# Scores ahead of the transposes in each step: one block moved in a fused attention and mixture-of-experts kernel

## The chip, the cores and the metric

The kernel runs on one core of one Trainium2 chip. Its time is the device time of one execution in microseconds (us). Several executions are run, and their median is quoted. A separate execution was taken by the hardware profiler; every duration of a single instruction below comes from that one. The engines are named as in the profile: PE is the matrix engine (TensorE), PEld its weight loads, DVE is VectorE, ACT is ScalarE, POOL is GpSimd and SP is SyncE, which here only issues DMA transfers.

## The reference

Two layers are computed, one after the other. The first is attention over 8 batches, 8 heads, 576 positions and 64 dimensions, in a causal window of 128 positions with a distance penalty. The second is a mixture of 8 experts over all 4608 tokens of 512 values, with a dense branch added.

```python
scores = scale * np.matmul(q, k.transpose(0, 1, 3, 2))
mask = (rel >= 0) & (rel < window)                       # window = 128
scores = np.where(mask, scores + bias[None], -1000000000.0)
attn = np.exp(scores - np.max(scores, axis=-1, keepdims=True))
attn = attn / (np.sum(attn, axis=-1, keepdims=True) + 1e-09)
x = np.matmul(attn, v)                                   # then to (4608, 512)

y_dense = np.maximum(x @ w1_dense, 0.0) @ w2_dense
logits = x @ w_gate
expert_idx = np.argmax(logits, axis=1)
gate_w = softmax(logits)[np.arange(N), expert_idx]
for e in range(8):                                       # each token by its one expert
    y_moe[mask] = gate_w[mask, None] * (np.maximum(x[mask] @ w1[e], 0.0) @ w2[e])
return y_dense + y_moe
```

## The kernel before

**Two stages.** In the first stage (to about 286 us) attention, the dense branch and the routing run together. In the second, 43 blocks of 128 rows go through the experts: `block` gathers the rows by DMA, does two layers and scatters the sum to the output. The dense pieces of the last batch run between the first blocks.

**Steps.** The first stage is a loop over 48 steps, `steps = [(u, pr) ...]`. A unit `u` is half the heads of one batch, so a batch is two units and six steps. A unit has three steps: `pr` 0 and 1 handle two blocks of 128 keys each (tiles of 128x1024 for two pairs of heads), `pr` 2 the last, short block (tiles of 128x128). The work on one pair `(u, pr)` is spread over several passes of the loop:

- In pass n, `scores` (L384) puts the mask and the key-query products of step n into two PSUM tiles `sq` (16 matmuls at L405, then 16 or 8 at L417), and ACT turns each into `p32` by one `Exp` (L428). The function `lo` that it returns subtracts the upper half of the bits on DVE (`plo`, L447). It is called at the end of the pass.
- In pass n+1, `attend` (L458) multiplies these by V into the one PSUM tile `ax` (L481: 48, 36 or 24 matmuls).
- In pass n+2, `norm` (L490) divides by the sums on DVE (L496, L497). This frees `ax`.
- In pass n+3, `flip` (L511) transposes the result on PE into a PSUM tile `tp` (L524) and ACT copies `tp` twice: to `xT` in fp32 for the routing and to `xTb` in bf16 for the dense branch (L531).

**Work between.** `items` and `gates` hold the routing and the dense branch of the batch that was last finished, cut into pieces. In pass n the first item runs between `norm` and `attend`, the others behind `attend`. Over the six passes of a batch they are: the gate product `gate_a` (`lp`, L546) and its reader on DVE `gate_av` one pass later; `gate_b` (`lg`, L571); `gate_c` (`pc`, L605, L613), read by `gate_d` one pass later; eight `dense1` (`hp`, L691, four matmuls each, read by ACT's `Relu` at L698); five `dense2` (`yp`, L706, read by ACT's copy at L714 and then scattered by POOL, L715).

**PSUM.** `sq` has one buffer for each of its two tiles and `ax` has one. All of `tp`, `lp`, `lg`, `pc`, `hp` and `yp` come from one pool, `psum_m`, with the tag `misc` and two buffers. A buffer is handed on when the last reader of its tile has been written down in the program; the instruction that fills it next waits for that reader. So while `lp` or `pc` waits for its reader in the next pass, one buffer alone goes round.

**Order.** The queues of PE, ACT and DVE stand exactly in the order in which the Python code emits them (`manual_schedule`, L1010), as does SP's queue up to pass 48 (L1027). POOL's order is chosen by the framework's scheduler. At the end of a pass stand the loads and turns of the next units: `turn` on DVE (L162), and on ACT `round_qk`, which makes `kT` (L172, in `pr` 1) and `qT` (L169, in `pr` 2). `qT` has a single buffer, and the scores of the next unit's `pr` 0 read it.

Of the kernel before, what the change touches and what calls it, by code (L numbers as in the profile page):

```python
# [23 lines left out]
def kernel(  # L24
# [100 lines left out]
    def load_k(u):  # L125
        b, hq = divmod(u, HQ)
        t = ld.tile([P, R, 2, 32], F32, name="kraw", tag="kraw")
        nc.sync.dma_start(
            out=t.rearrange("p r c d -> p (r c d)"),
            in_=k[b, 4 * hq : 4 * hq + 4].rearrange("h (p r) d -> (h p) (r d)", r=R),  # L130
        )
        raw[("k", u)] = t
# [26 lines left out]
    def turn(u, nm):  # L159
        t = raw.pop((nm, u))  # L160
        s = stg.tile([P, 2, S], F32, name=f"{nm}s", tag=f"{nm}s")
        nc.vector.transpose(out=s.rearrange("p c (r x) -> p r c x", r=R), in_=t)  # L162
        tmp[(nm, u)] = s

    def round_qk(u, nm):
        s = tmp.pop((nm, u))
        if nm == "q":
            d = qtp.tile([P, 2, S], F32R, name="qT", tag="qT", bufs=1)
            nc.scalar.copy(out=d, in_=s)  # L169
        else:  # L170
            d = kTs[u % 2]
            nc.scalar.copy(  # L172
                out=d[:, :, 0:S].rearrange("p c (x r) -> p c x r", r=R),
                in_=s.rearrange("p c (r x) -> p c x r", r=R),
            )
        qkT[(nm, u)] = d
# [69 lines left out]
    def mask_consts():  # L246

        nc.vector.tensor_single_scalar(
            out=far_i, in_=d_i, scalar=7, op=ALU.logical_shift_right
        )  # L250
        nc.vector.scalar_tensor_tensor(
            out=dist, in0=far_i, scalar=FAR, in1=d_i, op0=ALU.mult, op1=ALU.max
        )

        ax = psum_ax.tile([P, 2, 512], F32, name="ax", tag="ax")
        hp = psum_m.tile([P, 512], F32, name="hp", tag="misc")
        turned.extend((dist, ax[:, 0, :], ax[:, 1, :], hp))
        for g in range(1, 4):
            nc.tensor.matmul(
                out=turned[g],  # L260
                lhsT=ident2[:, P - 32 * g : 2 * P - 32 * g],
                rhs=dist,
                start=True,
                stop=True,
            )
# [3 lines left out]
    def mask_head(h):  # L269
        slope = 2.0 ** (-8.0 * (h + 1) / H)  # L270
        nc.scalar.activation(
            out=mask[:, h, :], in_=turned[h % 4], func=ACT.Copy, scale=-slope / SCALE
        )

    def mask_rest():
        for h in range(4, H):
            mask_head(h)
# [447 lines left out]
    def dense_items(b):  # L725
        one = [lambda c=c, h=h: dense1(b, c, h) for h in range(2) for c in range(4)]
        two = [lambda t=t: dense2(b, t) for t in range(NT)]
        return [one[0:2], one[2:4], two[0:2], one[4:6], one[6:8], two[2:5]]
# [10 lines left out]
    steps = [(u, pr) for u in range(NU) for pr in range(3)]  # L739
    NS = len(steps)  # L740
# [269 lines left out]
    with tc.manual_schedule(engines={ENG.PE, ENG.Activation, ENG.DVE}):  # L1010
        mask_consts()
        turn(0, "k")
        for h in range(4):
            mask_head(h)
        round_qk(0, "k")
        more_constants()
        mask_rest()
        turn(0, "q")
        round_qk(0, "q")
        load_k(1)  # L1020
        load_q(1, nc.sync)
        norms, gates, items = {}, {}, {}
        wnext = 0
        jm = 0
        n = 0
        loads = ExitStack()
        loads.enter_context(tc.manual_schedule(engines={ENG.SP}))  # L1027
        while jm < NB:
            if n == NS:
                loads.close()  # L1030
            if n > NS + 1:
                def middle():
                    if n - 2 in norms:
                        norms.pop(n - 2)()
                    for f in gates.pop(n, []):
                        f()
                    if n - 3 < NS:
                        flip(*steps[n - 3])

                block(jm, [middle] + items.pop(n, []))  # L1040
                jm += 1
            if 0 <= n - 3 < NS:
                if n <= NS + 1:
                    flip(*steps[n - 3])
                u2, pr2 = steps[n - 3]
                b2 = u2 // HQ
                if pr2 == 2:
                    items.setdefault(n, []).append(lambda u=u2: gate_a(u))
                    gates.setdefault(n + 1, []).append(lambda u=u2: gate_av(u))
                if u2 % HQ == HQ - 1 and pr2 == 2:  # L1050
                    for i, f in ((1, gate_b), (2, gate_c)):
                        items.setdefault(n + i, []).append(lambda f=f, b=b2: f(b))
                    for i, f in ((2, gate_bv), (3, gate_d)):
                        gates.setdefault(n + i, []).append(lambda f=f, b=b2: f(b))
                    for i, fs in enumerate(dense_items(b2)):
                        items.setdefault(n + 2 + i, []).extend(fs)
                    if b2 == NQ - 1:
                        gen = route_early()
                        for i in range(5):
                            gates.setdefault(n + 4 + i, []).append(  # L1060
                                lambda g=gen: next(g, None)
                            )
                        gates.setdefault(n + 9, []).append(early_used)
                    if b2 == B - 1:
                        gen = late_table()
                        part = lambda: next(gen, None)
                        for i, f in enumerate(
                            (late_counts, part, late_fill, part, part, part)
                        ):
                            gates.setdefault(n + 4 + i // 2, []).append(f)  # L1070
            lo = None
            if n < NS:
                u, pr = steps[n]
                lo = scores(u, pr)
            if n - 2 in norms:
                norms.pop(n - 2)()
            for f in gates.pop(n, []):
                f()
            if n == 0:
                prep_v(0)  # L1080
            todo = items.pop(n, [])
            for f in todo[:1]:
                f()
            if 0 <= n - 1 < NS:
                norms[n - 1] = attend(*steps[n - 1])
            for f in todo[1:]:
                f()
            if n < NS:
                if pr == 0:
                    if u + 1 < NU:  # L1090
                        turn(u + 1, "k")
                        if u + 2 < NU:
                            load_k(u + 2)
                elif pr == 1:
                    if u + 1 < NU:
                        round_qk(u + 1, "k")
                        turn(u + 1, "q")
                        if u + 1 + 1 < NU:
                            load_q(u + 1 + 1, nc.sync)
                else:  # L1100
                    if u + 2 < NU:
                        load_v(u + 2)
                    if u + 1 < NU:
                        round_qk(u + 1, "q")
                        prep_v(u + 1)
            if lo:
                lo()
            if n == 0:
                load_v(1)
            while wnext < 2 * (E + 1) and n < NS and wnext <= 18 * (n - 4) / 42:  # L1110
                pace(wnext)
                load_weights(wnext)
                wnext += 1
            if n == NS + 1:
                ph1.close()
                mpool = ctx.enter_context(
                    tc.tile_pool(name="mpool", bufs=3, reuse_waits="tile")
                )
                psum_t, psum_h, psum_y = [
                    ctx.enter_context(  # L1120
                        tc.tile_pool(
                            name=nm,
                            bufs=2,
                            space=bass.MemoryType.PSUM,
                            reuse_waits="tile",
                        )
                    )
                    for nm in ("psum_t", "psum_h", "psum_y")
                ]
                for j in range(AHEAD + 1):  # L1130
                    fetch(j)
            n += 1
        assert wnext == 2 * (E + 1)
# [30 lines left out]
```

## Time and profile before

| What | Value |
|---|---|
| Median of 3 executions | 434.8 us (432.84 to 435.57) |
| The profiled execution: its time | 435.34 us |
| Its span, first to last instruction | 433.6 us |
| Busy share of the span: PE, PEld, DVE, ACT, POOL | 81%, 51%, 65%, 60%, 46% |
| Mean granted PE clock | 0.93 of full speed |
| `Exp` of a 128x1024 tile (L428) | 1025 ns, 64 of them |
| Copy of a 128x512 `tp` to `xT`, to `xTb` (L531) | 588 ns, 596 ns, 32 of each |
| `plo` of a 128x1024 tile (L447) | 1236 ns, 64 of them |
| First `xr` load of the second stage issued by SP | 288.54 us |

In the lines shown further on, a timeline row has the start in us, the duration of the merged run in us, engine, source line, operation and tiles, the count, and in brackets the idle time of the engine before the row with what ended it. A waits row reads "engine, tile, line <- what it waited for: us in total, times, longest". A windows row has a stretch of the span, its length, and for each engine the busy us with the count of instructions, then the granted clock, the DMA share and GB/s. Matmuls are pipelined and their ends are modelled, so the runs of neighbouring matmuls overlap a little.

### The profile page before, as it was taken

What the parts mean: (1) busy time and instruction counts of PE and PEld (TensorE: products, weight loads), DVE (VectorE), ACT (ScalarE), POOL (GpSimd) and SP (SyncE); (2) the same over time, 40 slices, a digit from 0 to 9 for tenths busy, and PEclk for the clock granted to TensorE, in tenths of its full rate; (3) what the DMA queues carried; (4) which work ended last, traced back from release to release, by engine and by line L of the source; (5) the groups of instructions that cost most, each with busy time, mean ns of one, the idle gap of its engine ahead of it and who ended that gap; (6) DMA issues with size and microseconds to landing.
All of it is one profiled execution on the core that took longest, in us unless ns stands there. A gap on an engine that the chain in (4) does not pass through costs nothing.

```text
span 433.6 us, 12269 instructions
## 1 busy us (share of the span) xinstructions
PE 350.9 (81%) x4659; PEld 220.0 (51%) x4659; DVE 279.7 (65%) x541; ACT 261.1 (60%) x431; POOL 197.6 (46%) x245
## 2 busy tenths in 40 slices
PE   3547689898897898879879878758949899999990
PEld 0435466556566456466556545533525455555550
DVE  5579987788787788577887969711425244454440
ACT  6538854787786787467687677533424555555550
POOL 4023134445764665644567554360453534444341
PEclk9969985999899998889999899996988999999997
DMA  4657687878777969669669573138768789889820
GB/s 143 178 129 156 165 166 159 226 162 207 212 176 218 224 162 234 169 193 216 130 190 217 200 178 50 63 126 286 241 218 295 251 245 290 242 245 249 281 98 13
DMA packets 84986, 82.40 MB, mean 190 GB/s; under 512 B 43583, under 2 KB 71615, under 8 KB 84928
## 3 DMA queue, kind: packets, MB, share of 16 engines
q1 hardware_dynamic: 66852, 48.17, 39.9%
q0 software_dynamic: 17680, 33.12, 30.0%
q8 instruction: 38, 0.62, 0.6%
q10 hardware_dynamic: 396, 0.33, 0.2%
q14 instruction: 20, 0.16, 0.1%
HBM read 64.20 MB, written 28.66 MB: 214 GB/s over the span
## 4 chain that ended last, share of the span: by engine, by line
PE 35%; DVE 14%; issue 13%; DMA 12%; POOL 9%; ACT 6%; another core or an unknown queue 5%; SPq 2%; POOLq 1%; ACTq 0%; DVEq 0%
PE ax L481 8%; POOL out_dram L975 8%; DVE plo L447 8%; PE yp L706 6%; DMA qraw<-in_q_dram 6%; PE hp L691 5%; PE tp L524 3%; DMA vf<-in_v_dram 3%; ACT p L428 3%; PE sq L417 3%; DVE qs L162 2%; DVE xf L497 2%; PE lp L546 2%; PE lg L571 2%
## 5 line engine op out<-in xcount | busy, mean ns | idle before, releaser
L447 DVE TENSOR_TENSOR plo<-p 128x1024 bf16<-128x1024 f32 (+1 forms) x96 | 86.5, 941 | 26.5 <-ACT p L428 22.1
L428 ACT ACTIVATE p<-sq 128x1024 f32<-128x1024 f32 (+1 forms) x96 | 69.7, 783 | 22.8 <-remote 6.2
L481 PE MATMUL ax<-vf,p 128*128 128x65 bf16 (+1 forms) x576 | 69.6, 206 | 16.8 <-DVE xf L497 13.4
L481 PEld LDWEIGHTS <-p 128*128 128x128 bf16 (+1 forms) x1152 | 65.7, 108 | 29.9 <-DVE xf L497 17.4
L975 POOL DMA_INDIRECT out_dram<-yo,xr x43 | 42.4, 986 | 75.8 <-DVE yo L974 66.8
L503 POOL CAST xrow<-xf 128x512 bf16<-128x512 f32 (+1 forms) x48 | 34.9, 732 | 81.5 <-DVE xf L497 75.1
L481 PE MATMUL ax<-vl,p 128*128 128x64 bf16 (+1 forms) x576 | 68.9, 203 | 1.9 <-issue 1.8
L481 PE MATMUL ax<-vf,plo 128*128 128x65 bf16 (+1 forms) x576 | 69.0, 204 | 0.9 <-issue 0.6
L715 POOL DMA_INDIRECT ys_dram<-yt,slot x40 | 48.0, 1200 | 27.3 <-ACT yt L714 17.7
L481 PEld LDWEIGHTS <-plo 128*128 128x128 bf16 (+1 forms) x576 | 59.3, 107 | 1.6 <-issue 1.0
L691 PE MATMUL hp<-xTb,w_all 128*128 128x256 bf16 (+1 forms) x256 | 45.8, 308 | 14.3 <-ACT hTd L698 6.8
L966 PE MATMUL y<-w_all,hTm 128*128 x172 | 45.3, 386 | 8.1 <-ACT hTm L958 7.3
L924 DVE COPY xTm<-xps 128x512 bf16<-128x512 bf16 x43 | 18.2, 424 | 51.7 <-PE xps L918 29.6
L645 POOL DMA_INDIRECT xs_dram<-xrow,slot x40 | 43.1, 1077 | 17.0 <-issue 11.1
L698 ACT ACTIVATE hTd<-hp 128x256 bf16<-128x256 f32 (+1 forms) x64 | 26.6, 418 | 39.8 <-PE hp L691 31.7
L939 PE MATMUL hpm<-w_all,xTm 128*128 x172 | 45.7, 389 | 2.7 <-DVE xTm L924 1.2
L974 DVE TENSOR_TENSOR yo<-y,yr 128x512 f32<-128x512 f32 x43 | 29.7, 691 | 23.8 <-PE y L966 21.4
L706 PE MATMUL yp<-w_all,hTd 128*128 128x512 bf16 (+1 forms) x160 | 42.4, 393 | 1.9 <-DVE ltsb L560 1.0
L947 ACT ACTIVATE hr<-hpm,xr 128x512 bf16<-128x512 f32 x43 | 29.6, 687 | 21.9 <-PE hpm L939 10.5
L958 ACT COPY hTm<-hps 128x512 bf16<-128x512 bf16 x43 | 25.1, 585 | 28.4 <-PE hps L954 23.6
L531 ACT COPY xT<-tp 128x512 f32<-128x512 f32 (+1 forms) x48 | 23.1, 482 | 23.1 <-PE tp L524 19.7
L524 PE MATMUL tp<-ident_f,xf 128*128 128x128 f32 (+1 forms) x160 | 27.6, 289 | 11.3 <-ACT yt L714 6.6
(146 smaller groups left out, 573.3 us busy)
## 6 DMA issues: line engine op xcount, KB each, us to landing
yr<-ys_dram SPq DMA_DIRECT2D x43, 256.0 KB
kraw<-in_k_dram SPq DMA_DIRECT2D x16, 576.0 KB
vf<-in_v_dram SPq DMA_DIRECT2D x64, 128.0 KB
w_all<-in_moe_w_dram POOLq DMA_DIRECT2D x16, 512.0 KB
qraw<-in_q_dram SPq DMA_DIRECT2D x62, 128.0 KB
xr<-xs_dram SPq DMA_DIRECT2D x43, 130.0 KB
ys_dram<-fill_x SPq DMA_DIRECT2D x8, 256.0 KB
xs_dram<-fill_x SPq DMA_DIRECT2D x8, 130.0 KB
```

Of the source, the lines that this page charges most:

```text
L428: nc.scalar.activation(out=p32[:, :, 0:tot], in_=sq[i][:, :, 0:tot], func=ACT.Exp, scale=SCALE,)
L447: nc.vector.tensor_tensor(out=plo[:, :, 0:tot], in0=p32[:, :, 0:tot], in1=phi[:, :, 0:tot], op=ALU.subtract,)
L481: nc.tensor.matmul(out=ax[:rows, i, o0 : o0 + w], lhsT=lhs, rhs=rhs, start=(n == 1), stop=(n == 3 * len(kl)),)
L503: nc.gpsimd.tensor_copy(out=xrow[:rows, qis[0] : qis[0] + nt, hq * 256 : hq * 256 + 256], in_=xf[:rows, 0:nt],)
L524: nc.tensor.transpose(out=tp[:, i, c, 0:rows], in_=xf[:rows, i, c * P : c * P + P], identity=ident_f[:rows, :rows],)
L645: ins = nc.gpsimd.indirect_dma_start(out=xs_dram[:, :], out_offset=bass.IndirectOffsetOnAxis(ap=slot[:rows, t : t + 1], axis=0), in_=xrow. ...
L691: nc.tensor.matmul(out=hp[:, 0:HF], lhsT=w_all[:, E, 0, kc, c * P : c * P + P], rhs=xTb[:, kc, c0:c1], start=(kc == 0), stop=(kc == 3),)
L706: nc.tensor.matmul(out=yp[:rows, :], lhsT=hT[:, c, t0 * P : t0 * P + rows], rhs=w_all[:, E, 1, c, :], start=(c == 0), stop=(c == 3),)
L715: ins = nc.gpsimd.indirect_dma_start(out=ys_dram[:, :], out_offset=bass.IndirectOffsetOnAxis(ap=slots[b][:rows, t : t + 1], axis=0), in_=y ...
L939: nc.tensor.matmul(out=hp, lhsT=xT[:, kc, :], rhs=w_all[:, bass.DynSlice(er, 1), 0, kc, :], start=(kc == 0), stop=(kc == 3),)
L966: nc.tensor.matmul(out=y, lhsT=hT[:, c, :], rhs=w_all[:, bass.DynSlice(er, 1), 1, c, :], start=(c == 0), stop=(c == 3),)
L975: ins = nc.gpsimd.indirect_dma_start(out=out[:, :], out_offset=bass.IndirectOffsetOnAxis(ap=xr.bitcast(I32)[:, TC : TC + 1], axis=0), in_= ...
```

## The change

The block that emits `scores` of step n moves up in the pass. It stood behind `flip` of step n-3 and the code that files the next items; it now stands ahead of them.

```diff
                 block(jm, [middle] + items.pop(n, []))
                 jm += 1
+            lo = None
+            if n < NS:
+                u, pr = steps[n]
+                lo = scores(u, pr)
             if 0 <= n - 3 < NS:
                 if n <= NS + 1:
                     flip(*steps[n - 3])
...
                             gates.setdefault(n + 4 + i // 2, []).append(f)
-            lo = None
-            if n < NS:
-                u, pr = steps[n]
-                lo = scores(u, pr)
             if n - 2 in norms:
                 norms.pop(n - 2)()
```

In passes 3 to 47, PE's queue then holds mask and scores of step n, the transposes of step n-3, the first item, `attend` of step n-1 and the other items. ACT's queue holds the two `Exp` of step n, then the two copies of `tp`, then the readers of the items. No instruction is added or taken away. Passes 0 to 2 have no `flip`, and from pass 48 on there are no scores, so these are as before. The queues of DVE and SP are unchanged, instruction for instruction. On POOL the scheduler moves the second or third `ys` scatter of a batch (L715) behind the next copy of `xrow` (L503) or behind the start of a weight load (L734, L89).

## The prediction

> **What bounds the kernel now.** I read four views: the chain that ended last, the windows by stage, PE's waits, and ACT's timeline of one batch. First the chain:
>
> ```profile
> PE 35%; DVE 14%; issue 13%; DMA 12%; POOL 9%; ACT 6%; another core or an unknown queue 5%; SPq 2%; POOLq 1%; ACTq 0%; DVEq 0%
> ```
>
> PE is the largest part, but no engine holds the chain alone. The change acts in passes 3 to 47, from 31 to 278 us. The windows of that stretch:
>
> ```profile
> 25.00:145.00 120.00, 99.53 (x1765) 69.72 (x1766) 100.72 (x162) 83.11 (x134) 56.49 (x65) 0.90 0.76 181
> 145.00:265.00 120.00, 102.02 (x1713) 67.78 (x1713) 93.44 (x164) 86.49 (x146) 66.89 (x77) 0.94 0.75 185
> ```
>
> PE is busy for 201.6 of 240 us, DVE 194.2, ACT 169.6. The stage is a loop of in-order queues with little slack: a new PE wait that nothing overlaps lengthens it. PE's waits from 25 to 265 us:
>
> ```profile
> PE ax L481 <- DVE xf L497: 13.4, 8, 6.1
> PE tp L524 <- ACT yt L714: 6.6, 6, 1.5
> PE hp L691 <- ACT hTd L698: 5.0, 6, 1.4
> PE hp L691 <- ACT xTb L531: 0.3, 1, 0.3
> ```
>
> The first three rows are what exists now. The last matters most: `hp` takes over the PSUM buffer of `tp` once `xTb` is copied, and pays 0.3 us in the whole stage. ACT's timeline shows why:
>
> ```profile
> 196.11 1.15 ACT L169 CAST qT<-qs 128x1152 fp32r<-128x1152 f32 x1
> 197.15 0.59 ACT L531 COPY xT<-tp 128x512 f32<-128x512 f32 x1
> 197.63 0.60 ACT L531 CAST xTb<-tp 128x512 bf16<-128x512 f32 x1
> 198.10 1.96 ACT L428 ACTIVATE p<-sq 128x1024 f32<-128x1024 f32 x2
> 199.92 0.62 ACT L714 COPY yt<-yp 128x512 f32<-128x512 f32 x1
> ```
>
> The copies run at 197.15 to 198.23, while PE does the scores (to 198.05). `Exp` starts 0.05 us after the scores. So the copies are free now, and the buffer is back when PE wants it.
>
> [...]
>
> **The change part by part.** No instruction is added, so the cost is all waits. I work through the batch from 196.34 to 229.08 us (passes 33 to 38), with PE's start-to-start distances there: four transposes 0.59 us (two: 0.27), mask 0.37, `yp` 0.97, `pc` 0.17, `hp` 0.45 to 0.55, `ax` of 24, 36, 48 matmuls 0.89, 1.22, 1.49.
>
> When is `tp`'s buffer free? Let s be the end of the scores. `Exp` starts at s+0.05, the next ACT row comes 1.82 later (198.10 to 199.92), `xTb` follows `xT` by 0.48 and takes 0.59, the signal 0.05: free at s+3.0. PE issues its next instruction at s-0.07 and reaches the one that takes over this buffer:
>
> - Passes with `yp` (33, 36): transposes 0.59, first `yp` 0.97 (the other buffer), `ax` 0.89: s+2.4. The second `yp` waits 0.6, twice per batch: 1.2.
> - Pass 34: `pc` takes the other buffer and keeps it. Transposes, `pc`, `ax`: s+1.9. `hp` waits 1.1.
> - Pass 37: transposes, first `hp` 0.55, `ax` (here 1.13): s+2.2; the second `hp` waits 0.8.
> - Short passes (35, 38): ACT does `kT` before everything. With e the end of the previous `hp`, its `Relu` ends at e+0.42; `kT`, both `Exp` and both copies end 2.74 later (208.28 to a reordered 211.02), so free at e+3.2. PE needs mask and scores 0.52, transposes 0.27, `hp` 0.45, `ax` 1.49, from e-0.1: e+2.6. The second `hp` waits 0.6, twice: 1.2.
> - `qT` (33, 36): it ends at 197.25 and 213.58. Scores now go first, so PE stands at L417 at 196.34+0.37 and 212.72+0.36. It waits 0.6 and 0.55, where the transposes were the cover: 1.1.
>
> Added: 1.2+1.1+0.8+1.2+1.1 = 5.4 us per batch. Removed: `Exp` and thus `plo` start about 0.9 us earlier in their pass, which ends the wait of `ax` for `xf` in pass 38 (0.71) and of `hp` for `basee` in pass 35 (0.38). The transposes no longer lead, so their wait for a `Relu` in pass 35 (0.47) hides behind scores, and their wait for `yt` in pass 37 mostly does too (it is 1.49; I count 0.2, since the rest follows from a late `Exp`, below). In pass 34 the second `hp` gains 0.3 (ACT is free when the first ends). Sum 2.1. Net: 5.4-2.1 = 3.3 us per batch of six passes.
>
> The late `Exp`: once per batch (79.59, 112.22, 146.03, 181.31, 216.66, 251.74) the first `Exp` starts some 2 us after the modelled scores (216.66 against 214.42), while PE goes on. The trace does not show the cause. Before, it costs PE the 1.49 at `yt` next pass, 1.3 over what I counted. After, if it stays, the copies wait too, and the second `yp` waits 2.2 more: 0.9 more per batch. If it vanishes, 2.2 of today's batch time go. I take nothing for it and keep +0.9 and -2.2 for the range.
>
> The dense branch fills passes 12 to 45: 5.5 batches times 3.3 = 18.2. Passes 10 and 46 are like 34 (0.8 each), 11 and 47 like 35 (-0.25 each): +1.1. Passes 3 to 9 have few items; an earlier `Exp` saves perhaps 0.5 there, since `turn` already waits for the `q` transfer at 50.05 and 65.13 (0.6 and 0.8). Sum 18.8. [...] so 18.
>
> What else moves: the later `ys` scatters on POOL cost nothing, as `yt` has four buffers; without that cover each would hold a `yt` copy by some 1.2 us (mean of L715). SP's order is the same; its loads of V wait for PE's `ax` and shift with it. After pass 47 all is as before: SP's first `xr` load (288.54) follows the last `ax` (285.40), so the lateness passes on one for one. The profiled execution took 435.34: 435.3+18 = 453.3. Against the median, 434.8+18, I say **453 us**.
>
> **The rivals.** (1) The wait for `xTb` as above, 447 to 459: for it speaks that the built program has `hp` and `yp` wait for ACT's count behind `xTb`, with no third buffer. Chance 0.70.
>
> (2) The wait comes, but the late `Exp` vanishes or other slack takes part of it: 5.5 times 2.2 is 12, so 453-12 = 441, in 439 to 447. For it: its place is in the scores, which move. Against: nothing that precedes it on PE's side goes away. 0.15.
>
> (3) The change does nothing measurable, 434.8 within 1%: the second buffer would have to be free when PE needs one, in passes where I count it held. Against it: `lp` and `pc` are read one pass later. 0.06.
>
> (4) Faster. One mechanism: `Exp`, `plo`, `norm`, `ax` is the loop that decides, and it starts 0.96 us earlier (two copies). It could win back the waits of `ax` for `xf` (13.4, of which 6.1 stand ahead of the first moved pass: 7.3), so 434.8-7 = 428. It decides only if PE's waits for `xTb` stay under 7.3 in the stage, 0.2 per pass. I count 0.55 to 1.1 in each. 0.04.
>
> (5) Slower still, over 459: the new gaps lower the granted clock. [...] this trace cannot tell, it has 0.93 in the mean with dips. If it fell by 0.07 in the stage, 201.6 times 0.07 = 14 us of PE time, half of it exposed: 453+7 = 460. 0.05.
>
> **How the numbers follow.** 453 is the likeliest case; its own range is 447 to 459. 443 to 460 takes the likeliest, half of (2) and a little of (5): about 0.8. A measurement of this kernel tells about 1% from no change (430.5 to 439.1). Slower by over 1%: (1)+(2)+(5) = 0.90; within: 0.06; faster: 0.04.
>
> **What would show it.** In PE's waits `hp` and `yp` for ACT `xTb` should rise from 0.5 to 20 to 30 us, some 35 times; `sq` L417 should wait for `qT` (0.6, some 13 times); `ax` for `xf` should fall. ACT's `xT` should follow the second `Exp` directly, and `tp` should wait little for `yt` and `hTd`. A pass from 34 to 45 should be 0.5 us longer in the mean, and the first `xr` load stand near 306. The prediction is wrong if `xTb` stays under 7 us among PE's waits, or if a batch keeps its 33 to 34 us.

## The result, and the profile after

The changed kernel takes 457.6 us in the median of four executions (454.2 to 464.1), the kernel before 434.5 (432.8 to 435.6). The ratio is 1.051, with a 95% interval of 1.040 to 1.062: slower. The profiled execution of the changed kernel took 454.2 us with a span of 452.5 us, against 435.3 and 433.6 before. The medians differ by 23.1 us, the two spans by 18.9, and it is this second difference that the traces can explain. Disturbed executions (that of 464.1 us, and some of the later sessions) are left out of the ratios.

The chain that ended last, in the changed kernel:

```profile
PE 30%; issue 18%; ACT 13%; DVE 10%; POOL 10%; DMA 9%; SPq 6%; POOLq 1%; ACTq 0%; DVEq 0%
```

PE's share fell from 35% to 30%, ACT's rose from 6% to 13%: work of ScalarE that stood beside the chain has moved onto it. The windows of the first stage (stretch, length, busy time of PE, PEld, DVE, ACT and POOL, then the granted clock, the DMA share and GB/s):

```profile
25.00:145.00 120.00, 93.91 (x1653) 67.59 (x1654) 97.06 (x156) 78.95 (x125) 50.05 (x62) 0.93 0.73 175
145.00:265.00 120.00, 95.55 (x1566) 65.51 (x1564) 82.61 (x144) 78.26 (x134) 59.27 (x69) 0.92 0.74 178
```

PE is busy for 189.5 of the 240 us, 12.1 less than before, and all other engines are less busy too: the same work has been spread over a longer stage. The granted clock is about what it was (0.90 and 0.94). PE's waits from 25 to 285 us (total, times, longest):

```profile
PE hp L691 <- ACT xTb L531: 14.6, 17, 1.9
PE yp L706 <- ACT xTb L531: 14.4, 10, 2.7
PE ax L481 <- DVE xf L497: 7.7, 4, 5.4
PE sq L417 <- ACT qT L169: 7.3, 11, 1.4
PE hp L691 <- ACT hTd L698: 3.2, 6, 0.5
```

The wait for `xTb` was 0.5 us in this window; it is now 29.0 us in 27 places. The wait for `qT` is new. The waits for `xf` and `hTd` have shrunk, and the one for `yt` (6.6 us) is gone. ACT's timeline in pass 33, one of the six that the prediction worked through, shows how such a wait comes about, here that of `yp` in the second row:

```profile
205.58 1.14 ACT L169 CAST qT<-qs 128x1152 fp32r<-128x1152 f32 x1
207.62 1.94 ACT L428 ACTIVATE p<-sq 128x1024 f32<-128x1024 f32 x2 [0.89 <-PE sq L417]
209.44 0.59 ACT L531 COPY xT<-tp 128x512 f32<-128x512 f32 x1
209.91 0.62 ACT L531 CAST xTb<-tp 128x512 bf16<-128x512 f32 x1
210.38 0.64 ACT L714 COPY yt<-yp 128x512 f32<-128x512 f32 x1
```

Before, `xTb` was copied while PE still did the scores. Now ACT waits 0.89 us for the scores, does both `Exp`, and copies last; `xTb` ends at 210.53. PE's second `yp`, which fills the buffer that this copy empties, starts at 210.57, after 0.72 us of idling. It had wanted to start at 209.85.

### The profile page after: what moved, and what is told of

Its sections match the earlier page's. It is cut to its first block, busy times and chain, and to the rows that moved or that the text cites. A ratio compares the mean times of both kernels' runs of the same rounds, so it can differ in the third digit from the quotient of the medians.

```text
span 452.5 us, 12298 instructions
## 1 busy us (share of the span) xinstructions
PE 355.1 (78%) x4659; PEld 227.1 (50%) x4659; DVE 279.0 (62%) x541; ACT 262.4 (58%) x431; POOL 189.7 (42%) x245
## 4 chain that ended last, share of the span: by engine, by line
PE 30%; issue 18%; ACT 13%; DVE 10%; POOL 10%; DMA 9%; SPq 6%; POOLq 1%; ACTq 0%; DVEq 0%
POOL out_dram L975 8%; PE yp L706 6%; DMA qraw<-in_q_dram 6%; PE hp L691 6%; PE ax L481 5%; PE sq L417 4%; ACT p L428 3%; DVE plo L447 3%; PE tp L524 3%; ACT kT L172 2%; ACT xT L531 2%; DVE qs L162 2%; ACT xTb L531 2%; ACT qT L169 2%; PE lg L571 2%
## 5 line engine op out<-in xcount | busy, mean ns | idle before, releaser
L447 DVE TENSOR_TENSOR plo<-p 128x1024 bf16<-128x1024 f32 (+1 forms) x96 | 84.6, 922 | 30.0 <-ACT p L428 27.7
L481 PEld LDWEIGHTS <-p 128*128 128x128 bf16 (+1 forms) x1152 | 67.2, 110 | 21.5 <-issue 10.7
L503 POOL CAST xrow<-xf 128x512 bf16<-128x512 f32 (+1 forms) x48 | 36.4, 758 | 94.3 <-DVE xf L497 87.8
L481 PEld LDWEIGHTS <-plo 128*128 128x128 bf16 (+1 forms) x576 | 60.5, 109 | 1.3 <-DVE plo L447 1.1
L715 POOL DMA_INDIRECT ys_dram<-yt,slot x40 | 40.3, 1009 | 43.4 <-ACT yt L714 34.6
L706 PE MATMUL yp<-w_all,hTd 128*128 128x512 bf16 (+1 forms) x160 | 43.4, 402 | 17.9 <-ACT xTb L531 14.4
L417 PE MATMUL sq<-qT,kT 32*128 32x256 f32 (+2 forms) x640 | 34.2, 321 | 15.2 <-ACT qT L169 14.2
L947 ACT ACTIVATE hr<-hpm,xr 128x512 bf16<-128x512 f32 x43 | 29.5, 687 | 24.1 <-PE hpm L939 10.5
L691 PEld LDWEIGHTS <-w_all 128*128 128x128 bf16 x256 | 24.7, 103 | 31.9 <-issue 25.0
```

The costliest lines, as they stand in the source:

```text
L417: nc.tensor.matmul(out=sq[g // 2][:, g % 2, i * wid : i * wid + nq], lhsT=kT[32 * g : 32 * g + 32, c, kj * P : kj * P + P], rhs=qT[32 * g ...
L447: nc.vector.tensor_tensor(out=plo[:, :, 0:tot], in0=p32[:, :, 0:tot], in1=phi[:, :, 0:tot], op=ALU.subtract,)
L481: nc.tensor.matmul(out=ax[:rows, i, o0 : o0 + w], lhsT=lhs, rhs=rhs, start=(n == 1), stop=(n == 3 * len(kl)),)
L503: nc.gpsimd.tensor_copy(out=xrow[:rows, qis[0] : qis[0] + nt, hq * 256 : hq * 256 + 256], in_=xf[:rows, 0:nt],)
L691: nc.tensor.matmul(out=hp[:, 0:HF], lhsT=w_all[:, E, 0, kc, c * P : c * P + P], rhs=xTb[:, kc, c0:c1], start=(kc == 0), stop=(kc == 3),)
L706: nc.tensor.matmul(out=yp[:rows, :], lhsT=hT[:, c, t0 * P : t0 * P + rows], rhs=w_all[:, E, 1, c, :], start=(c == 0), stop=(c == 3),)
```

## The experiments

All kernels below were made from the changed kernel or the one before. They ran in three sessions, each on one chip, beside runs of the kernel before. Call the pair above session A. The first four kernels ran in session C (the kernel before: 410.2 us), the next four in session B (440.2), the last four in session D (410.9). So the same kernel differs by up to 7% between sessions. Each of these sessions had a chip of its own (that of A is not on record), so chip and session can't be told apart, and a time is read only against the kernel before of its own session. Expectations written with 434.5 in mind are read as distances from the kernel before.

### Each half alone

First the half on TensorE alone: `flip` stands between the matmuls of `scores` and its two `Exp`.

```diff
         ps = []
+        if pre:
+            pre()
         for i in range(2):
...
+                pre = None
+                if n >= 3:
+                    pre = lambda: flip(*steps[n - 3])
-                lo = scores(u, pr)
+                lo = scores(u, pr, pre=pre)
```

> Only the half on TensorE: scores ahead of the transposes, but on ScalarE both copies ahead of both Exp. Theory (hand-over of the transposed tiles' buffer): with s the end of the scores, transposes 0.59, signal 0.05, copies 0.48+0.59, signal 0.05 give the buffer back at s+1.75, before PE needs it (s+1.9 to s+2.4). So hp and yp should wait for xTb under 4 us in all (29.0 in the changed kernel), the wait at L417 for qT stays near 7, and the time is 438 to 445. Rival (the loop Exp, plo, norm, ax has no slack): Exp starts 1.7 us later than in the changed kernel, so PE's waits move to ax (for plo or xf) by over 15 us and the time is 450 to 458, although the xTb waits are gone.

Measured: 433.3 us, ratio 1.056 (1.047 to 1.065). PE's waits, and the first of ACT's, from 25 to 285 us:

```profile
PE ax L485 <- DVE xf L501: 11.4, 8, 6.2
PE sq L405 <- ACT p L432: 8.7, 14, 1.3
PE hp L695 <- ACT hTd L702: 8.2, 6, 1.6
PE hp L695 <- DVE basee L634: 5.5, 6, 1.0
PE sq L417 <- ACT qT L169: 5.2, 12, 0.5
```

```profile
ACT xT L535 <- PE tp L528: 56.2, 29, 6.8
```

No `xTb` row is left, as the hand-over theory said, yet the kernel is 23 us slower than before. The theory's time (4 to 10 us over) is refuted. The rival has the cost right (16 to 24 over), but not the place: `ax` waits 11.4 us for `xf`, and 13.4 before in A. ACT's copies wait for the transposes behind the scores, so `Exp` starts 1.6 us after the end of the scores in most passes, and the mask of the next step must wait for `sq`, whose single buffers `Exp` reads (8.7 us), and `hp` for readers that stand behind it. These waits are not the whole cost. The last `attend` ends at 301.1 us, 24.6 later than in the hybrid of session D (below), which has the order of before from pass 10 on; 12.0 of these are PE's busy time (233.6 against 221.6 us up to there), which no experiment here explains.

Then the half on ScalarE alone: transposes ahead of the scores as before, both `Exp` ahead of the copies.

```diff
+                cp = flip(*steps[n - 3]) if n >= 3 else None
                 lo = scores(u, pr)
+                if cp:
+                    cp()
```

Here `flip` does the transposes and returns the function that emits the copies.

> Only the half on ScalarE: PE keeps the transposes ahead of the scores, ScalarE has both Exp ahead of the copies. Theory (hand-over): the buffer comes back at s+3.0 as in the changed kernel, but PE no longer has the transposes between scores and hp/yp, so it needs it 0.59 earlier (0.27 in short passes): 2.9 us more waiting per batch, less 1.1 for qT, and the waits of tp for hTd and yt return (1.5 or so): 5.5 batches times about 1.8 to 3.3 over the changed kernel, 464 to 472, xTb waits 38 to 50 us. Rival (the scores' new place on PE, with qT and the late Exp, is the cost): 434 to 440, since that place is undone.

Measured: 432.3 us, ratio 1.053 (1.041 to 1.064), 22 us over the kernel before. The profiled execution took 438.0 us, more than the median; its waits:

```profile
PE hp L694 <- ACT xTb L534: 18.6, 18, 1.6
PE yp L709 <- ACT xTb L534: 13.2, 11, 1.2
```

The wait for `xTb` comes back with ScalarE's order alone (31.8 us in 29 places, less than the 38 to 50 expected), and the wait at L417 is gone. The cost is less than the 30 to 38 us of the theory, too. The rival, that the scores' place on PE is the cost, is refuted. Each half alone costs 22 to 23 us. Both together cost half of that in session D, where the kernel before takes 410.9 us after 410.2 here (next part): their costs don't add. The lists suggest why: with both, the mask waits 0.3 us for `Exp` instead of 8.7, and the waits for `xTb` are 23.4 us instead of 31.8 (the changed kernel in D).

### The whole change, and the buffer earlier

The changed kernel was run again in sessions B and D, without any edit.

> The changed kernel once more, beside the kernel before on the chip of the first four experiments, where the kernel before takes 410.2 us and its late Exp (the signal of the scores 2 to 3.5 us after their modelled end) is not seen in the four traces. Theory (hand-over; the late Exp counted as neutral in the sum): 18 us over the kernel before here too, about 428, with 20 to 30 us of waits of hp and yp for xTb. Rival (a good part of the 5% on the first chip came from the late Exp, which the change makes dearer, 0.9 per batch): 5 us less, 421 to 424. Rival (the ratio is a ratio of clocks): 1.05 times 410 = 431, with waits that don't add up to it.

It fell into session B, on another chip than it was written for. Its four executions lie from 456.6 to 474.5 us there, against 440.2, and give no ratio. In session D:

> The changed kernel, beside the split order and the kernel before on one chip, since the chips differ (the kernel before takes 410 us on one, 434 and 440 on two others). Theory (hand-over): 16 to 20 us over the kernel before on whichever chip, ratio 1.04 to 1.05, xTb waits 20 to 30 us. Rival (the late signals of TensorE make the cost): ratio 1.04 to 1.05 only where the late signals are seen, and 1.02 or less where they are not.

Measured in D: 421.7 us against 410.9, ratio 1.025 (1.011 to 1.039). It is slower here too, but the interval ends just below the 1.040 at which that of session A begins: the size depends on the chip or the session. The hand-over theory's ratio of 1.04 to 1.05 is too much here. The rival's "1.02 or less" lies partly inside the interval and isn't excluded.

Now ScalarE does the first `Exp`, both copies, and the second `Exp`, with PE's order of the changed kernel. By my estimate the buffer comes back some 0.9 us earlier, half of the 1.82 us from the first `Exp` to the copy of `xT` (203.49 to 205.31 in pass 34 of the changed kernel in D).

```diff
         for i in range(2):
+            if i == 1 and mid:
+                mid()
             p32 = ppool.tile([P, 2, tot], F32, name="p32", tag=f"p32_{tot}", bufs=4 if len(kjs) == 2 else 2)
...
+                mid = None
+                if n >= 3:
+                    mid = lambda: flip(*steps[n - 3])
-                lo = scores(u, pr)
+                lo = scores(u, pr, mid=mid)
```

> The changed kernel's order on PE, and on ScalarE first Exp, both copies, second Exp. Theory (hand-over): buffer back at s+0.05+0.92+0.48+0.59+0.05 = s+2.1, 0.9 earlier than in the changed kernel, so 4.3 us of xTb waits per batch fall to about 0.3; qT's 1.1 stays: xTb waits 2 to 8 us in all, time 438 to 447. Rival (loop over Exp, plo, ax without slack): the second Exp ends 1.1 later, half of the gain is lost at ax, 447 to 454. Rival (the buffer isn't the cause): 455 to 460.

> The split order of the third experiment (first Exp, both copies, second Exp) beside the changed kernel on one chip. Theory (hand-over): 10 to 14 us less than the changed kernel on the same chip, xTb waits 2 to 8 us. Rival (late signals make the cost): on a chip with them the copies stand behind the late first Exp as before, so it gains 5 us or less on the changed kernel.

Measured: in C 418.4 us, ratio 1.016 (1.004 to 1.028); in D 418.0, ratio 1.017 (1.009 to 1.024). That is 7 to 8 us over the kernel before, within what the theory gave (4 to 12). PE's waits in D:

```profile
PE ax L485 <- DVE xf L501: 11.5, 8, 6.0
PE hp L695 <- DVE basee L634: 8.9, 6, 5.2
PE sq L417 <- ACT qT L169: 6.0, 12, 0.5
...
PE sq L405 <- ACT p L432: 3.9, 4, 1.3
...
PE hp L695 <- ACT xTb L535: 2.0, 8, 0.5
```

The `xTb` waits fall from 23.4 us (the changed kernel in D) to 2.0, as expected. But the whole kernel hardly gains: the median is 3.7 us lower, where 10 to 14 were expected, and the intervals of the two ratios (1.009 to 1.024, and 1.011 to 1.039) overlap, so no gain in the time is shown. The rival of the last expectation speaks of a chip with a late `Exp`, and D shows none (below), so it stays open.

The traces tell more. Windows from the mask of pass 12 to that of pass 42, five batches, in the changed kernel and in the split order, both in D:

```profile
75.02:248.19 173.17, 142.65 (x2472) 99.37 (x2480) 135.86 (x229) 126.74 (x211) 92.78 (x111) 0.96 0.80 197
75.88:242.35 166.47, 141.66 (x2472) 98.86 (x2480) 133.69 (x226) 123.55 (x211) 95.86 (x110) 0.96 0.82 201
```

In this stretch the earlier buffer saves 6.7 us, and the split order takes no longer than the order of before (166.7 us, see the table further on; 165.0 in the trace of C). So in these passes the growth goes with the late return of the buffer; counted by the shortest passes alone (further on), about half of it does. The `xTb` waits fall by 18.3 us: for the most part they stood in place of other waits, which come back at `basee` and `xf`. Outside it the gain is lost again, and the two spans differ by only 0.3 us: 0.9 us ahead of pass 12, 3.4 between pass 42 and the end of the last `attend`, where the second `yp` of pass 45 waits 3.0 us for `ltsb` of DVE in both traces of the split order (1.3 in the changed kernel), and 2.7 in the second stage. Why is open.

Next, the changed kernel with `xTb` made on POOL from `xT`, so that one copy of ScalarE alone holds the buffer.

```diff
-        for dst in (cur["xT"], cur[("xTb", b)][:, 2 * hq : 2 * hq + 2, :]):
+        for dst in (cur["xT"],):
...
+        nc.gpsimd.tensor_copy(
+            out=cur[("xTb", b)][:, 2 * hq : 2 * hq + 2, q0 : q0 + nt * rows],
+            in_=cur["xT"][:, :, q0 : q0 + nt * rows],
+        )
```

> The changed kernel with xTb made on POOL from xT, so that one ScalarE copy alone holds the buffer and Exp keeps its place ahead. Theory (hand-over): buffer back at s+2.5, 0.5 to 0.6 earlier: of 4.3 us per batch 1.2 stay, so 3 times 5.5 = 17 less than the changed kernel, 438 to 445, xTb waits near 0 and hp/yp waits for xT 5 to 10 us. Rival (the loop Exp to ax is the cost): Exp's place is the same, 453 to 459.

Measured in C: 412.8 us, ratio 1.005 (1.002 to 1.008). That is 2.5 us over the kernel before, where the theory had 3.5 to 10.5.

```profile
PE hp L695 <- ACT xT L531: 6.1, 15, 0.6
...
PE yp L710 <- ACT xT L531: 2.7, 10, 0.7
```

The waits for the buffer are 8.8 us, within the 5 to 10 expected, and with `Exp` ahead of the copy the cost is 2.5 us here, where the changed kernel cost 10.8 in D. Since this edit also takes 0.48 us of work per pass from ScalarE, it got a control in session B: the kernel before with the same edit.

> A control for the fourth experiment: the kernel before, with xTb made on POOL. It has no xTb waits to lose, so by the hand-over theory it gains nothing: 409 to 412 (Exp 0.48 earlier behind one copy). Rival (the fourth experiment gained by taking 0.48 us of work per pass off ScalarE, not by the buffer): it falls by as much as the changed kernel did, to 395 to 402.

Measured in B: 449.3 against 440.2 us, ratio 1.020 (1.007 to 1.033). It neither stays nor falls: it costs 9 us on this chip. So less work on ScalarE brought no gain by itself there. But the control ran on another chip than the kernel that it belongs to, so how much of the gain in C is the buffer and how much the shorter queue is not settled.

In the same session, the changed kernel with `xTb` on POOL and `round_qk(u + 1, "q")` emitted right behind `flip` in the third pass of a unit:

> The changed kernel with xTb on POOL and the rounding of the next q moved up on ScalarE, to right behind xT of the third pass of a unit, so that it is ready before the next unit's scores. Theory: the two waits that the change added (xTb and qT) are then both gone; the L417 wait for qT (5.0 us) falls to 0, and of it some 2 to 4 us arrive in the time: 409 to 411, no slower than the kernel before. Rival: the 1.15 us of ScalarE now stand ahead of the Relu, the second hp waits for hTd or its buffer instead, and the time stays at 412 to 414.

Measured in B: 461.9 us, ratio 1.049 (1.034 to 1.065). The wait for `qT` is gone from the list, but not the time:

```profile
PE yp L710 <- ACT xT L531: 11.3, 11, 2.0
PE hp L695 <- ACT xT L531: 10.7, 12, 1.6
```

PE waits 22.0 us for the buffer here, against 8.8 for the same copy in C. Both theories put the time far too low. In this trace the first `Exp` of passes 12, 18, 24, 30, 36 and 42 starts 1.4 to 4.4 us after the modelled end of its scores, which is the next part.

### The late Exp

> The kernel before once more, for its profile on the chip of the first four experiments: the time is 410 and its trace should show whether the 24 us against the first chip (434.8) lie in the late signals of TensorE in the stage from 25 to 285 us (theory: 7 passes by 2 to 3 us, so 12 to 20 of the 24), or in the second stage, after 300 us (rival: the records of the split kernel show 272 GB/s there against 253).

It too fell into session B, where it took 435.0 us, so it shows the kernel before on a chip like that of A. Its first `Exp` is late by 2.3 to 3.8 us in passes 12, 18, 24, 30, 36 and 42, as in A (2.0 to 3.5). The expectations call this a late signal of TensorE; the traces show the late start of `Exp` alone. In session D no trace shows a late `Exp` in these passes, nor in C. There the stretch from pass 12 to pass 42 of the order of before takes 166.7 us, against 171.2 in A; 13.8 us more are saved behind the last `attend`, in the second stage. So most of the 22.7 us between the two spans lie in the second stage, and the rival holds.

ScalarE in pass 36 with the order of before, first the control of session B, then the hybrid of session D (below):

```profile
222.11 0.59 ACT L531 COPY xT<-tp 128x512 f32<-128x512 f32 x1
228.01 1.94 ACT L428 ACTIVATE p<-sq 128x1024 f32<-128x1024 f32 x2 [5.31 <-remote]
```

```profile
210.69 0.59 ACT L531 CAST xTb<-tp 128x512 bf16<-128x512 f32 x1
211.18 1.94 ACT L428 ACTIVATE p<-sq 128x1024 f32<-128x1024 f32 x2
```

In B `Exp` starts at 228.01, after 5.31 us of idling, though the modelled end of its scores is 222.85; in D it follows them at once. The five `xs_dram` scatters of POOL run from 220.8 to 226.8 in the first of them. To see whether the late `Exp` goes with them, they were emitted one pass later in the kernel before.

```diff
-                    for i, f in ((2, gate_bv), (3, gate_d)):
+                    for i, f in ((2, gate_bv), (3, gate_d), (4, gate_x)):
```

Here `gate_x` holds the loop of the five scatters.

> The kernel before with the five scatters into xs_dram of each batch issued one pass later. Theory on the late Exp (POOL's scatters hold up TensorE or its signals): on a chip that has it, the first Exp starts 2 us or more late in passes 13, 19, 25, 31, 37, 43 instead of 12, 18, 24, 30, 36, 42. Rival (it belongs to TensorE's instructions of those passes): it stays in 12, 18, 24, 30, 36, 42. On a chip without it nothing moves: within 3 us of the kernel before.

It ran in session D: 411.7 us, and the late `Exp` is absent there anyway. The first scatter of pass 36 also stands only 1.3 us later than in the hybrid (206.0 to 207.3), and the pass itself 0.9. The run says nothing on the cause.

### The new order where nothing takes the buffer over

```diff
+            if 3 <= n and 10 <= n <= NS + 1:
+                flip(*steps[n - 3])
             if n < NS:
                 u, pr = steps[n]
                 lo = scores(u, pr)
...
-                if n <= NS + 1:
+                if n < 10:
```

> The changed order only in passes 3 to 9, where no hp or yp follows, and the order of before from pass 10. Theory: no xTb waits (under 1.5 us), and the 1 to 1.4 us that the changed kernel was ahead at passes 9 and 11 stay: 0 to 2 us less than the kernel before. Rival (the gain at the start is given back at the loads of q and v, which DVE waits for there): equal to before within 0.3%.

Measured in D: 412.0 us, ratio 1.0036 (1.0005 to 1.0067). In A the changed kernel was ahead by 1.0 us at the mask of pass 9 and by 1.4 at that of pass 11; in D no such gain is in the time. In A the lead goes with the clock: up to pass 9 the kernel before had a granted clock of 0.92 and the changed one 1.00, from pass 9 to 12 they had 0.70 and 0.89. No version here beats the kernel before.

## Why the prediction was right, and where it was not

Foretold were 453 us, in 443 to 460; measured were 457.6. For the profiled execution 18 us were foretold, and the spans differ by 18.9. The step that decides is right: the buffer of `tp` comes back later, and PE waits for it. That the total came so near is partly luck, as the parts show.

The five batches from the start of pass 12 to that of pass 42 are the best place for a sum. The order of before in D is that of the hybrid. PE's waits in these stretches, for before and after in A:

```profile
PE tp L524 <- ACT yt L714: 5.5, 5, 1.5
PE hp L691 <- ACT hTd L698: 4.5, 5, 1.4
...
PE tp L524 <- ACT hTd L698: 3.6, 6, 1.3
PE ax L481 <- DVE xf L497: 1.9, 3, 0.7
PE hp L691 <- DVE basee L630: 1.9, 5, 0.4
```

```profile
PE yp L706 <- ACT xTb L531: 13.2, 9, 2.7
PE hp L691 <- ACT xTb L531: 12.8, 14, 1.9
PE sq L417 <- ACT qT L169: 5.4, 9, 0.9
PE hp L691 <- ACT hTd L698: 2.7, 5, 0.5
```

And for the hybrid and the changed kernel in D:

```profile
PE hp L691 <- DVE basee L630: 8.8, 5, 4.0
PE ax L481 <- DVE xf L497: 6.0, 5, 2.5
PE hp L691 <- ACT hTd L698: 3.2, 5, 0.8
PE tp L524 <- ACT hTd L698: 2.4, 5, 0.5
```

```profile
PE hp L691 <- ACT xTb L531: 12.1, 17, 1.1
PE yp L706 <- ACT xTb L531: 7.2, 10, 0.7
PE sq L417 <- ACT qT L169: 4.8, 10, 0.5
PE tp L524 <- DVE basee L630: 3.0, 1, 3.0
PE hp L691 <- ACT hTd L698: 2.7, 5, 0.5
```

| Pass 12 to 42 (us) | before, A | after, A | hybrid, D | after, D | split, D |
|---|---|---|---|---|---|
| Length | 171.2 | 191.0 | 166.7 | 173.2 | 166.5 |
| PE busy | 148.1 | 152.9 | 143.6 | 142.7 | 141.7 |
| Waits for `xTb` and `qT` | 0.3 | 31.4 | 0 | 24.1 | 6.0 |
| All other waits listed | 22.2 | 6.4 | 22.3 | 5.7 | 18.0 |
| Granted clock | 0.95 | 0.92 | 0.93 | 0.96 | 0.96 |

Now the prediction's steps in turn.

- **The buffer comes free at s+3.0.** Right. In D a pass like 34 has its first `Exp` at 203.49 and `xTb` ending at 206.40, and `hp` waits 1.11 us (1.1 predicted). The second `yp` waits 0.71 and 0.72 (0.6), the pass like 37 has 0.74 (0.8), the short passes 0.46 and 0.16 (0.6 each), `qT` 0.52 and 0.47 (0.6 and 0.55).
- **Added waits, 5.4 us per batch.** Right in size: 31.1/5 = 6.2 in A, 24.1/5 = 4.8 in D. The 27 waits for `xTb` and 29.0 us in A lie in the 20 to 30 us foretold, with fewer places than 35.
- **Removed waits, 2.1 us per batch.** Too small. The other waits fall by 15.8/5 = 3.2 in A and 16.6/5 = 3.3 in D. In A the term that failed is `tp` for `yt`, counted at 0.2: it went wholly (5.5/5 = 1.1). In D PE waits more for `basee` and `xf` of DVE before, and these waits mostly go. Some of them are waits for transfers, which the prediction left out. In the stretch of the hybrid, DVE waits:

```profile
DVE qs L162 <- DMA qraw<-in_q_dram: 7.0, 3, 4.0
DVE qs L162 <- DMA vf<-in_v_dram: 3.5, 1, 3.5
```

Behind the longest of each, DVE works without a pause up to the sum `basee`, for which `hp` then waits 4.0 and 3.7 us (passes 23 and 35). In A no wait of DVE for a transfer is listed in this stretch.
- **Net 3.3 per batch.** In A the stage grew by 19.8/5 = 4.0, of which 3.1 are waits and 1.0 is PE's busy time, at a granted clock of 0.92 after 0.95. That the forecast's 18.8 became 18 was an estimate that the clock would rise, which no trace had shown; in these batches it fell. The agreement of 3.3 and 3.1 is partly luck: added and removed were both too small by about 1. In D the net of the waits is 1.5, and the growth 1.3. But a batch made up of the shortest pass of each of its six kinds takes 29.3 us in the hybrid, 33.0 in the changed kernel and 31.1 in the split order. So where nothing else holds up a pass, the change costs 3.7 per batch in D too, near the 3.3 foretold. The sum of 5.5 batches also left out pass 45, which grew by 0.9 in A and 0.6 in D.
- **The late `Exp` counted as nothing.** Near enough in A, as a sum: the waits for `yt` that it caused before (5.5 us in five) went, and in its place four `yp` waits are 2.0 to 2.7 us long instead of 0.7. But the step says nothing of the chip: in D, without the late `Exp`, the change costs half. That it accounts for the whole gap between A and D was not isolated. Up to the last `attend` the change costs 24.8 us in A and 8.2 in D. Of the 16.6 between them 7.9 are PE's busy time, which grew by 6.4 in A and fell by 1.5 in D, and the other 8.7 are time in which PE stood idle.
- **Passes 3 to 9, -0.5.** Not borne out: the hybrid gains nothing.
- **The lateness passes on one for one.** Not quite. At the mask of pass 12 the changed kernel was 3.6 us ahead in A, with a granted clock of 0.98 up to there against 0.87. The five batches added 19.8. The stretch behind pass 42, up to the last `attend`, added 8.6, where I had counted about 2; its clock was 0.89 against 1.00, and 4.4 of the 8.6 are PE's busy time. So the last `attend` ended 24.8 us later (285.40 to 310.15). From there to the end the kernel then took 5.8 us less: before, SP's first `xr` load stood 3.1 us behind the last `attend`, and the profile has it wait for an unknown queue; now it follows the `attend` at once. It stood at 310.2, not near 306. These errors largely cancel in the 18.9. In D the stretch behind pass 42 grew by 1.3.
- **The rivals.** (3) and (4) are refuted by the times. In (4), `ax` for `xf` did fall, from 13.4 to 7.7, but the `xTb` waits of 29.0 are far over the 7.3 at which it was to decide. (2) didn't happen in A: the late `Exp` stayed in five of the six passes. (5) is not seen over the whole stage, with 0.93 and 0.92 after 0.90 and 0.94, nor in the mean over the span, 0.937 after 0.930. That new gaps lower the clock was a conjecture of mine, and it is not shown. The five batches of A have 30.7 us at half clock in the changed kernel and 17.1 before. Windows of the changed kernel behind the wait of 2.4 us for `xTb` in pass 18, which ends at 117.42:

```profile
117.42:119.04 1.62, 1.62 (x28) 0.73 (x31) 1.52 (x4) 1.00 (x2) 1.42 (x2) 1.00 0.03 11
119.04:122.45 3.41, 3.41 (x40) 2.69 (x33) 2.39 (x3) 2.75 (x5) 2.42 (x3) 0.50 0.71 79
```

Seven waits for `xTb` in these batches last 1.9 to 2.7 us, and behind six of them the clock is halved (0.50) within 2.7 us of their end. In D the waits of the changed kernel are 0.2 to 1.1 us long from 145.93 to 241.50, 26 of them, and the clock stays at 1.00. No experiment isolates whether the one follows from the other, and the kernel before has five such halvings in its stretch with no wait over 1.5 us.

The forecast was right in its sign and its mechanism: the waits for `xTb` and `qT` appear where they were worked out, and about as long. What it left open is how much each stretch of waiting is worth: in the five batches the split order took 18.3 us of `xTb` waits away and saved 6.7 us.

## What to carry to other kernels

When an instruction is moved behind others on one engine, look up which buffer its completion returns and who fills that buffer next, and work out the moment from both sides; where `Exp` was not late, this gave most waits right to 0.2 us. Then ask which old waits stand behind the new one in the same loop, since these vanish with it: here two thirds of the new waiting in D (16.6 of 24.1 us), and half in A (15.8 of 31.1), only replaced old waiting. In D some of the old waits came from transfers. Two halves of a reordering must be costed together: each alone cost 5 to 6% (in C, the kernel before at 410.2 us), and both together 2.5% (in D, at 410.9).

## What the runs showed of the hardware that was not expected

The kernel before takes 410 to 411 us on two chips and 434 to 440 in the two other sessions, and the change costs 2.5% on one of the former and 5.1% in the first of the latter. In the slower sessions the first `Exp` of passes 12, 18, 24, 30, 36 and 42 comes 2 to 3.8 us after the modelled end of its scores; with one more POOL copy per pass it came up to 5.4 us late. PE's records go on meanwhile, with pauses under "issue" (12.9 us in 20 places at `ax` in that control). The delay falls into the time of POOL's scatters (220.8 to 226.8 us in pass 36 of that control), and in D `Exp` follows its scores at once in that pass, though the same scatters run (the first at 206.0, `Exp` at 211.18). What causes it is open. PE's busy time is the other surprise: for the same work of five batches it is 148.1 us at a granted clock of 0.95 before and 152.9 at 0.92 after in A, but 143.6 at 0.93 in the hybrid in D. So waits alone don't account for a time here, and the mean clock beside them doesn't either.
